# A list plan for the stretch between attention and the fast MLP tiles of a fused attention, Fourier-mixing and MLP kernel

## The chip, the cores and the metric

One core of one Trainium2 chip. The metric is device time in microseconds of one execution. Engines: TensorE (PE, with its weight loads PEld), VectorE (DVE), ScalarE (ACT), GpSimd (POOL) and SyncE (SP, which issues most DMAs).

## The reference

```python
bias = -(cum[:, :, :, None] - cum[:, :, None, :])         # cum: running sum of max(s, 0)
scores = where(causal, -1e9, q @ k.T / sqrt(64) + min(bias, 0))
x = softmax(scores) @ v                                   # 8 batches x 8 heads x 576 x 64
u = x + real(fft(fft(x, axis=seq), axis=model))           # 8 x 576 x 512
un = (u - mean(u)) / sqrt(var(u) + 1e-6)
out = u + max(un @ w_ch1, 0) @ w_ch2                      # 512 -> 2048 -> 512
```

All in float32; the kernel makes products nearly exact by splitting operands into a high and a low part and summing three products.

## The kernel before, in words

**Attention.** 32 pairs of heads (4 pairs for each of 8 batches). Iteration `i` of the loop at line 818 weaves the scores of pair `i`, the products with v of pair `i-1`, the row maxima (`pm`, line 685) of pair `i+1`, and, of earlier batches, the folds (`folds`, 470) and the Fourier products (`fourier`, 500: `pzs`, `pzc`, `pyc`, `pys`), whose result `u` goes to DRAM as `uD`. Each batch of 576 tokens becomes a run of rows of `uD`.

**MLP.** 4608 tokens in nine tiles of 512. A tile is normalised (`ln_tile`, 192), its four quarters split (`bh`, `bl`), and for each of 16 chunks `f` of the hidden 2048 there is a first product `h` (24 matmuls, 363), a relu split on ACT and DVE (`zh` 370, `zl` 371), and a second product into four PSUM accumulators (`acc`, 12 matmuls, 268 to 270). Tiles one and two run like that; tiles three to nine use a scheme with seven products in place of eight (`fast_tile`, 381, first matmul at 407).

**Weights** arrive as 64-bit numbers, in pieces of 128 x 256 (`raw`, 256 KB). A piece costs four DVE instructions (83, 85, 87, 88), one of ACT (84) and one of POOL (89), then a split into `wh` and `wl` (or, for the second matrix, `w2h` and `w2l`, whose split parts are kept in DRAM as `w2D` and loaded again for every tile). A chunk has four pieces, two of the first matrix and two of the second. Six chunks are converted in the shade of attention (`convert_w`), the other ten between the products of tiles one and two (`load_w`).

**Order.** Tiles one and two are cut in two phases because not all first matrices fit beside the Fourier buffers: chunks 0 to 7 of tile one, of tile two, then 8 to 15 of tile one, of tile two. The partial sum of the first phase goes through `uD` (`keeper`, 331: load, add, store). PE's order is that of the code: `weave` merges streams by rough shares. The other engines' orders are set by the framework's scheduler, which reorders within dependencies. All orders are fixed before the kernel starts.

## Time and profile before

| | |
|---|---|
| median of 3 runs | 1448.6 us (1447.39 to 1451.24) |
| profiled execution | 1449.54 us, its span 1447.8 |
| PE / DVE / ACT / POOL busy | 1291.8 / 865.7 / 630.1 / 523.3 us |
| mean granted TensorE clock | 0.954 |

Times in rows are microseconds from the span's start, durations of a single instruction in a group nanoseconds. In a group's row the part behind the second bar is idle time of the engine just before these instructions and what ended it. In a row of waits stand the total, the number and the longest. Matmuls overlap in the rows: the spacing of starts, not the length, is what one costs.

### The profile page before, as it was taken

The page shows a single profiled execution, that of the slowest core. Times are in us where ns is not written, and L with a number is a line of the kernel's source. Part 1 is how long each engine was busy: PE and PEld are TensorE (multiplying, and loading weights), DVE is VectorE, ACT ScalarE, POOL GpSimd, SP SyncE. Part 2 cuts the span into 40 slices and gives each one's busy share as a digit, 9 for nine tenths or more (in the row PEclk, how much of TensorE's full clock was granted, in tenths as well). Part 3 has the DMA queues.
Part 4 walks back from the last instruction along what each step waited for, and adds up shares of the span by engine and source line. Part 5 has one row for each costly group of instructions (what it writes and reads, how often), then busy time and mean ns, then how long its engine had stood idle before and what let it go on. Part 6 is the DMA issues. An engine that isn't in the chain of part 4 may idle for free.

```text
span 1447.8 us, 21997 instructions
## 1 busy us (share of the span) xinstructions
PE 1291.8 (89%) x7582; PEld 1124.5 (78%) x7582; DVE 865.7 (60%) x1989; ACT 630.1 (44%) x1472; POOL 523.3 (36%) x541
## 2 busy tenths in 40 slices
PE   4887979797988897488889989999999999999998
PEld 3676867686867685377769878888888898888987
DVE  6567676767676767586962778545445444554423
ACT  4665757566656556242431334333333333323321
POOL 6445464555556466544540444110211102021100
PEclk9998999898999998699989999999999999999999
DMA  8565556456655545446774433444435244452433
GB/s 198 139 179 148 140 159 180 132 156 180 154 165 142 166 123 184 170 144 200 225 239 146 137 135 103 147 132 129 161 103 185 92 146 146 124 168 88 140 123 116
DMA packets 130346, 218.68 MB, mean 151 GB/s; under 512 B 16985, under 2 KB 42009, under 8 KB 130235
## 3 DMA queue, kind: packets, MB, share of 16 engines
q1 hardware_dynamic: 127707, 213.18, 48.6%
q0 software_dynamic: 1712, 2.53, 0.9%
q10 hardware_dynamic: 816, 1.57, 0.3%
q8 instruction: 60, 0.98, 0.3%
q14 instruction: 51, 0.42, 0.1%
HBM read 159.72 MB, written 33.56 MB: 133 GB/s over the span
## 4 chain that ended last, share of the span: by engine, by line
PE 42%; DVE 7%; POOL 4%; DMA 4%; issue 4%; ACT 1%; SPq 0%; POOLq 0%; DVEq 0%; ACTq 0%
PE b L407 18%; PE acc L268 7%; PE acc L269 7%; PE acc L270 7%; DMA raw<-in_wP_dram 2%; PE h L363 1%; POOL we L89 1%; DMA w<-uD 1%; DVE wm L85 1%; DVE we L83 1%; DVE we L87 1%; DVE wm L88 1%; DMA u<-uD 1%; POOL w L315 1%; POOL t L216 0%
## 5 line engine op out<-in xcount | busy, mean ns | idle before, releaser
L268 PE MATMUL acc<-zh,w2h 128*128 128x512 f32 x576 | 230.4, 401 | 20.0 <-ACT zh L370 10.0
L270 PE MATMUL acc<-zl,w2h 128*128 128x512 f32 x576 | 230.6, 401 | 10.3 <-DVE zl L371 10.3
L269 PE MATMUL acc<-zh,w2l 128*128 128x512 f32 x576 | 231.3, 402 | 4.2 <-DMA w2l<-w2D 4.2
L749 PE MATMUL pavB<-P,va 128*128 128x320 f32 (+2 forms) x640 | 193.9, 397 | 10.0 <-ACT stage L753 9.6
L685 PE MATMUL pm<-KQ 128*128 128x256 f32 (+3 forms) x384 | 158.5, 432 | 44.2 <-DVE Mx L692 23.2
L721 ACT ACTIVATE P<-ps 128x320 f32<-128x320 f32 (+4 forms) x384 | 146.5, 393 | 117.2 <-PE ps L718 113.0
L315 POOL TENSOR_TENSOR w<-w,o 128x512 f32<-128x512 f32 x32 | 43.0, 1355 | 380.3 <-DVE o L311 342.7
L717 PE MATMUL ps<-KQ 128*128 128x256 f32 (+2 forms) x384 | 155.8, 408 | 19.7 <-ACT P L721 10.8
L692 DVE CUSTOM_DVE_ANT_0 trash<-pm,amask 128x128 bf16<-128x128 f32 (+3 forms) x256 | 123.7, 483 | 43.5 <-PE pm L685 26.9
L270 PEld LDWEIGHTS acc<-zl,w2h 128*128 128x128 f32 x576 | 110.4, 192 | 37.7 <-DVE zl L371 12.3
L268 PEld LDWEIGHTS acc<-zh,w2h 128*128 128x128 f32 x576 | 110.0, 191 | 29.0 <-ACT zh L370 10.5
L685 PEld LDWEIGHTS pm<-KQ 128*128 128x128 f32 x384 | 78.9, 208 | 65.2 <-DVE Mx L692 30.5
L749 PEld LDWEIGHTS pavB<-P,va 128*128 128x128 f32 x640 | 109.4, 200 | 19.3 <-ACT stage L753 14.1
L718 PE MATMUL ps<-Q,K 128*128 128x256 f32 (+2 forms) x384 | 121.9, 320 | 1.9 <-POOL Q L665 1.9
L399 ACT ACTIVATE zh<-cs 128x256 fp32r<-128x256 f32 x112 | 58.8, 525 | 142.8 <-DVE cs L419 88.7
L269 PEld LDWEIGHTS acc<-zh,w2l 128*128 128x128 f32 x576 | 110.7, 192 | 11.9 <-DMA w2l<-w2D 5.0
L665 POOL TENSOR_TENSOR Q<-qk,Q 64x576 fp32r<-64x576 f32 x64 | 100.2, 1580 | 39.8 <-DMA Q<-KQ 28.8
L717 PEld LDWEIGHTS ps<-KQ 128*128 128x128 f32 x384 | 77.5, 202 | 44.5 <-ACT P L721 17.0
L400 DVE SCALAR_TENSOR_TENSOR zl<-cs,zh 128x256 fp32r<-128x256 f32 x112 | 66.5, 594 | 69.2 <-ACT zh L399 69.2
L662 DVE TENSOR_TENSOR K<-qk,KQ 64x576 fp32r<-64x576 f32 x64 | 60.1, 940 | 75.9 <-ACT KQ L648 63.2
L407 PEld LDWEIGHTS b<-bh,wh 128*128 128x128 f32 x448 | 84.2, 189 | 24.3 <-DVE cs L419 4.8
L407 PE MATMUL b<-bh,wh 128*128 128x256 f32 x448 | 89.6, 281 | 3.5 <-DVE cs L419 3.5
(181 smaller groups left out, 2901.1 us busy)
## 6 DMA issues: line engine op xcount, KB each, us to landing
w2l<-w2D SPq DMA_DIRECT2D x136, 256.0 KB
w2h<-w2D SPq DMA_DIRECT2D x136, 256.0 KB
qk<-in_qkT_dram SPq DMA_DIRECT2D x32, 576.0 KB
raw<-in_wP_dram SPq DMA_DIRECT2D x64, 256.0 KB
...
```

Of the source, the lines that this page charges most:

```text
L268: nc.tensor.matmul(acc[j], a[:, cs], y, start=first, stop=False)
L269: nc.tensor.matmul(acc[j], b[:, cs], y, start=False, stop=False)
L270: nc.tensor.matmul(acc[j], a[:, cs], z, start=False, stop=final)
L400: nc.vector.scalar_tensor_tensor(out=y[1][:, at], in0=src, scalar=0.0, in1=y[0][:, at].bitcast(F32), op0=ALU.max, op1=ALU.subtract)
L407: nc.tensor.matmul(p[:, 0:256], a[:, j * 128:(j + 1) * 128], b[:, j], start=start and i == 0, stop=i == 5, skip_group_check=not start)
L665: nc.gpsimd.tensor_sub(q1[64:128, h], qk[0:64, h], q1[0:64, h].bitcast(F32))
L685: nc.tensor.matmul(p[:, :n], qy[:, h, 128 * c:128 * c + 128], ky[:, h, k0:k0 + n], start=True, stop=True)
L692: nc.vector.tensor_tensor_reduce(out=trash[:, :n], in0=p[:, :n], in1=amask[:, m0:m0 + n], scale=1.0, scalar=first if x else NEG, op0=ALU.a ...
L717: nc.tensor.matmul(p[:nk, :n], ky[:, h, ksl], qy[:, h, a:a + n], start=True, stop=False)
L718: nc.tensor.matmul(p[:nk, :n], k1[:, h, ksl], q1[:, h, a:a + n], start=False, stop=True)
L721: nc.scalar.activation(P[:nk, o:o + a + n - lo], p[:nk, lo - a:n], AF.Exp, scale=0.125)
L749: nc.tensor.matmul(p[:, a - lo:n], va[:nk, c, vs], P[:nk, o:o + w], start=c == 0, stop=c == cs[-1])
```

## The change

- Attention runs its loop for pairs 0 to 30, with all 24 pieces of the first six chunks spread over it and two buffers for them instead of one.
- Everything from pair 31 to the last chunk of tile two is written as generators. Each yields a step (engine, planned cost, what it needs, a buffer ring). `Flow.run` takes the step that can start first and, among those on its engine, the one with the earliest due time, and emits it. The plan's order is then kept on all engines; no scheduler reorders it.
- The first phase has six chunks (0 to 5) rather than eight. Conversion of chunks 6 to 15 is spread over the products. First halves of chunks 6 and 7 and all second halves have four staging buffers from attention's memory; first halves of chunks 8 to 15 have six, once the last Fourier is stored. Before there were three or four buffers.
- The first partial sum of tile one stays in four temporaries of the layer norm, with `u` added there; that of tile two is added to `u` in buffers fetched earlier and stays (three of four; one goes through `uD`).
- Tile one's `u` is loaded from SP's queue, not ACT's.

Three places in the order. The load of tile one's `u`: before, on ACT's queue among the exponentials (`P`) of pairs 30 and 31:

```order
L721 ACTIVATE P<-ps 128x320
L84 ACTIVATE we<-we,wbias 128x256
L753 COPY stage<-pavA 64x256
L721 ACTIVATE P<-ps 128x192
L721 ACTIVATE P<-ps 128x64
L195 DMA u<-uD 128x4x512
L69 CAST De_5887<-Df 128x289
```

Now, on SP's queue:

```order
L478 DMA uD<-xs 128x576
L695 DMA rb<-rd 64x576 x2
L625 DMA KQ_124<-mt 1x10x128
L477 DMA uD<-xa 128x2x576
L479 DMA uD<-xs 128x576
L683 DMA sums<-rows 16x1x36
L593 DMA va<-in_vA_dram 128x5x192
L1222 DMA u<-uD 128x4x512
L907 DMA rd<-sums 32x36
```

It moved behind three stores of `uD`, which wait for POOL, and behind the load of `va`, which waits for PE.

DVE where the late conversion begins. Before (`Do`, `De` belong to the last batch's fold, `wl` here are halves of chunks read back from DRAM):

```order
L371 SCALAR_TENSOR_TENSOR zl<-h,zh 128x512
L70 TENSOR_TENSOR Do_6480<-Df,Do_6479 128x288
L117 TENSOR_TENSOR wl_6561<-wl_6561,wh_6560 128x512
L482 TENSOR_TENSOR Df<-Aw 128x289
L117 TENSOR_TENSOR wl_6573<-wl_6573,wh_6572 128x512
L70 TENSOR_TENSOR De_6478<-Df,De_6477 128x289
L117 TENSOR_TENSOR wl_6585<-wl_6585,wh_6584 128x512
L486 TENSOR_TENSOR Df<-Bw 128x288
L83 TENSOR_SCALAR we<-raw 128x256
L85 TENSOR_SCALAR wm<-raw 128x256
```

Now:

```order
L955 TENSOR_TENSOR Do_6704<-Df,Do_6703 128x288
L980 TENSOR_TENSOR eh<-e,eh 1x289
L1110 TENSOR_SCALAR we<-raw 128x256 x2
L1301 SCALAR_TENSOR_TENSOR zl<-h,zh 128x512
L1267 RECIPROCAL r<-r 128x512
L1013 TENSOR_TENSOR zs_6878<-pz,zs_6877 96x256
```

Before, the first piece follows tile one's second `zl`; now it stands ahead of the sixth, and the first two instructions on a load are directly ahead of that `zl`.

DVE where the conversion ends. Before (`o` is an evacuation of an accumulator of tile two's first phase):

```order
L117 TENSOR_TENSOR wl_7587<-we,wh_7586 128x256
L338 TENSOR_TENSOR o<-r,acc_7641 128x512
L117 TENSOR_TENSOR wl_7587<-we,wh_7586 128x256
L83 TENSOR_SCALAR we<-raw 128x256
L85 TENSOR_SCALAR wm<-raw 128x256
L371 SCALAR_TENSOR_TENSOR zl<-h,zh 128x512
```

Now (`sx`, `s`, `sl` prepare the weights of the fast tiles):

```order
L1132 TENSOR_TENSOR wl_7339<-we,wh_7338 128x256
L1115 TENSOR_SCALAR wm<-raw 128x256
L1117 SCALAR_TENSOR_TENSOR wm<-raw,wm 128x256
L1120 SCALAR_TENSOR_TENSOR we<-raw,we 128x256
L1132 TENSOR_TENSOR wl_7341<-we,wh_7340 128x256 x2
L129 TENSOR_TENSOR sx<-sx 128x256
```

Before, the second halves of chunk 15 follow its `wl`, at the end of tile two's first phase; now `wl` of chunks 14 and 15 come last, after all second halves, with tile one in chunk 14.

```diff
-NC1 = 4.5
-N0 = 3
-N1 = 8
+N0 = 2
+N1 = 6
+NW = 8
+MARGIN = 1.5
+BACKLOG = 4.0
...
-    def keeper(t0, acc, r):
-        def done(j):
-            o = op.tile([128, TOK], F32, tag="o", name="o", bufs=2)
-            w = op.tile([128, TOK], F32, tag="w", name="w", bufs=3)
-            nc.sync.dma_start(out=w, in_=uD[j, :, t0:t0 + TOK])
-            nc.vector.tensor_mul(o, r, acc[j])
-            nc.gpsimd.tensor_add(w, w, o)
-            nc.sync.dma_start(out=uD[j, :, t0:t0 + TOK], in_=w)
-        return done
...
+    attb_ctx, attp_ctx, att_ctx, atop_ctx = (ExitStack() for _ in range(4))
     attb = attb_ctx.enter_context(tc.tile_pool(name="attb", bufs=1, side="right"))
-    psm = attb_ctx.enter_context(tc.tile_pool(name="psm", bufs=5, space=PSUM))
+    attp = attp_ctx.enter_context(tc.tile_pool(name="attp", bufs=1, side="right"))
...
-    weights = convert_w(attb, 0, NC, 1)
+    weights = convert_w(attb, 0, NC, 2)
...
+    for i in range(NP - 1):
...
+        share = NC * 4.0 / (NP - 1)
...
-            norm = chain(ln_tile(tiles[0], 6), plain(tiles[0]))
-            streams.append([take(norm, 10), 10 / 0.9])
...
-        for f in range(N0, N1):
-            yield from load_w(w1, f)
-        for _ in mixing:
-            yield 1.0
...
-    weave([plain_part(one, 0, N1, ready, early), N1], [chain(idle(1000), mixing), FOURIER * 0.6], [ahead(), 100],
-          [later(chain(ln_tile(two, 1), plain(two)), 2), 24])
...
-    STEPS = {(8, 0), (8, 3), (8, 4), (8, 5), (9, 2), (9, 3), (9, 4), (9, 5), *((10, x) for x in range(6)), (11, 0), (11, 1), (11, 3), (11, 5),
-             (12, 1), (12, 4), (12, 5), (13, 0), (13, 2), (13, 4), (14, 0)}
...
+    def piece(where, f, x, bufs, then):
+        e, rhold = yield dma(256, ring=(ring(where + "raw", bufs), 2))
+        home = stages[where]
+        raw = home.tile([128, 2 * WC], I32, tag="raw", name="raw", bufs=bufs)
+        nc.sync.dma_start(out=raw, in_=wP[f, :, WC * x:WC * x + WC].bitcast(I32))
+        hi = raw.rearrange("p (n w) -> p n w", w=2)[:, :, 1]
+        lo = raw.bitcast(U16).rearrange("p (n w) -> p n w", w=4)[:, :, 1]
+        e1, hold = yield ("DVE", 0.42, (e,), (ring(where + "we", bufs), 1))
+        n = home.tile([128, WC], I32, tag="we", name="we", bufs=bufs)
+        nc.vector.tensor_scalar(n, hi, 0x7FF00000, None, op0=ALU.bitwise_and)
+        e1 = yield act(400, e1)
+        nc.scalar.activation(n, n, AF.Relu, bias=wbias, scale=8.0)
+        _, mhold = yield ("DVE", 0.42, (e,), (ring(where + "wm", bufs), 1))
+        m = home.tile([128, WC], I32, tag="wm", name="wm", bufs=bufs)
+        nc.vector.tensor_scalar(m, hi, 0xFFFFF, 0x100000, op0=ALU.bitwise_and, op1=ALU.bitwise_or)
+        e = yield dve(256)
+        nc.vector.scalar_tensor_tensor(out=m.bitcast(F32), in0=lo, scalar=2.0 ** -16, in1=m, op0=ALU.mult, op1=ALU.add)
+        rhold.add(e)
+        e = yield dve(256, e1)
+        nc.vector.scalar_tensor_tensor(out=n, in0=hi, scalar=-0x80000000, in1=n, op0=ALU.bitwise_and, op1=ALU.bitwise_or)
+        rhold.add(e)
+        e = yield pool_(256, e)
+        nc.gpsimd.tensor_mul(n.bitcast(F32), m.bitcast(F32), n.bitcast(F32))
+        mhold.add(e)
+        yield from then(n.bitcast(F32), e, hold)
...
+            e = yield pool_(n, e) if pooled else dve(n, e)
+            (nc.gpsimd if pooled else nc.vector).tensor_sub(low[:, xs], v, h[:, xs].bitcast(F32))
...
+    def late_first(home, where, bufs, f0, f1):
+        for f in range(f0, f1):
+            wh = home.tile([128, 512], F32R, tag=f"wh{f}", name=f"wh{f}")
+            wl = home.tile([128, 512], F32R, tag=f"wl{f}", name=f"wl{f}")
+            W[f] = (wh, wl)
+            ready = Last(ev("W", f), 2)
+            for x in (0, 1):
...
+        e, hold = yield dma(1024, ring=(ring("lu", 1), 1))
+        u = lnp.tile([128, 4, TOK], F32, tag="u", name="u")
+        nc.sync.dma_start(out=u, in_=uD[:, :, t0:t0 + TOK].rearrange("c p t -> p c t"))
+        ev("lu", t0).hold = hold
...
+    parts = [(one_, 0, N1), (two_, 0, N1), (one_, N1, NF), (two_, N1, NF)]
+    last_of = [N1 - 1, 2 * N1 - 1, N1 + NF - 1, 2 * NF - 1]
+    todo = [(p, t0, f, f == f0, f == f1 - 1) for p, (t0, f0, f1) in enumerate(parts) for f in range(f0, f1)]
...
+    def evacuate(n, j, acc, e):
+        p, t0, f, _, _ = todo[n]
+        _, r = LN[t0]
+        if p:
+            e, ohold = yield ("DVE", 0.65, (e, ev("norm", t0)), (ring("oo", 2), 1))
+            o = op.tile([128, TOK], F32, tag="o", name="o", bufs=2)
+        else:
+            e, khold = yield ("DVE", 0.65, (e, ev("norm", t0)), (ring("lt", 4), 1))
+            o = lnp.tile([128, TOK], F32, tag="t", name="o", bufs=4)
+        nc.vector.tensor_mul(o, r, acc[j])
+        ev("acc", p, j).set(e)
+        if not p:
+            got, hold = yield dma(256, *at(*(("part", last_of[1], j) for j in range(4))), ring=(ring("oo", 2), 1))
+            w = op.tile([128, TOK], F32, tag="o", name="o", bufs=2)
+            nc.sync.dma_start(out=w, in_=uD[j, :, t0:t0 + TOK])
+            e = yield pool_(512, e, got)
+            nc.gpsimd.tensor_add(o, w, o)
+            hold.add(e)
+            kept[j] = (o, khold)
+            ev("part", n, j).set(e)
+            return
+        if p == 1:
+            yield wait(ev("fetched", j))
+            w, hold = ws[j]
+            e = yield pool_(512, e, ev("fetched", j))
+            nc.gpsimd.tensor_add(w, w, o)
+            ohold.add(e)
+            if j == 3:
+                e = yield dma(256, e)
+                nc.sync.dma_start(out=uD[j, :, t0:t0 + TOK], in_=w)
+                hold.add(e)
+            ev("part", n, j).set(e)
+            return
+        ev("rhold", t0).hold.add(e)
+        yield wait(ev("part", last_of[p - 2], j))
...
+                    flow.add(evacuate(n, j, acc[p], e), n - 900.0 + 0.1 * j)
...
+        for n, (p, t0, f, first, final) in enumerate(todo):
+            yield wait(ev("W", f), ev("plain", t0))
+            wh, wl = W[f]
+            bl = BL[t0]
+            e, hold = yield pe(12 * mm(256), ev("W", f), ev("plain", t0), ring=(ring("ps", 3), 1))
+            h = bank("h")
...
+            flow.add(relu_flow(h, hold, e, n), n - 900.5)
+            if n:
+                yield from second_product(n - 1)
...
+        yield wait(ev("out", L), *(ev("wD", f) for f in range(NC)))
+        attb_ctx.close()
+        stages["stage2"] = stage_ctx.enter_context(pool("stage2"))
+        late_first(w1, "stage2", 4, N1, NW)
+        flow.add(late_second(), 55.0)
+        yield wait(ev("u", B))
         fft_ctx.close()
         wB = ctx.enter_context(pool("wB", side="right"))
         op = ctx.enter_context(pool("op", side="right"))
...
+        late_first(wB, "stage3", 6, NW, NF)
...
+    for i in (L - 2, L - 1, L):
+        flow.add(close_pair(i), 3.0 + 8.0 * (i - L + 2))
+    flow.add(fourier_flow(B - 1, 14.0), 14.0, 1.0)
+    flow.add(folds_flow(B, 28.0), 28.0, 0.5)
+    flow.add(fourier_flow(B, 40.0), 40.0, 1.0)
+    flow.add(second_tile(), A0)
+    flow.add(fetch_u(), A0 + 60.0)
+    flow.add(second_loads(), mlp_due(N1) - 12.0, 1.87)
+    flow.add(mlp(), A0, 2.8)
+    flow.add(prepare(three_, C0 + 44.0), C0 + 44.0, 1.0)
+    flow.run(ev("first"), ev("prepared"), ev("sums_w"))
+    BL.pop(one_), BL.pop(two_)
     PLACES = {(0, 1), (1, 1), (1, 3), (1, 4), (1, 5), (2, 0), (2, 1), (2, 2), (2, 3), (2, 4), (2, 5), *((3, k) for k in range(7)),
...
+class Flow:
+    LAG = {"PE": 0.3, "ACT": 0.22, "DVE": 0.15, "POOL": 0.15}
+    def __init__(self):
+        self.free = dict.fromkeys(("PE", "ACT", "DVE", "POOL", "SP"), 0.0)
+        self.wire = 0.0
+        self.live = []
+    def add(self, gen, due, step=0.0):
+        self.send([gen, due, step, None], None)
+    def send(self, s, got):
+        new = s[3] is None
+        try:
+            s[3] = s[0].send(got)
+        except StopIteration:
+            if not new:
+                self.live.remove(s)
+            return
+        s[1] += s[2]
+        if new:
+            self.live.append(s)
+    def start(self, step):
+        engine, _, deps, ring = step
+        t = self.free[engine] if engine else 0.0
+        if ring:
+            deps = (*deps, ring[0].next())
+        late = MARGIN if engine == "SP" else 0.0
+        for d in deps:
+            if d.t is None:
+                return None
+            t = max(t, d.t + late)
+        return t
+    def run(self, *goals):
+        while any(g.t is None for g in goals):
+            ready = [(t, s) for s in self.live for t in (self.start(s[3]),) if t is not None]
+            if not ready:
+                raise RuntimeError("the plan is stuck: " + str([(s[0].__qualname__.split(".")[-1], s[1]) for s in self.live]))
+            t, s = min(ready, key=lambda x: (x[1][3][0] is not None, x[0]))
+            engine = s[3][0]
+            t, s = min(((u, v) for u, v in ready if v[3][0] == engine and u <= t + 0.05), key=lambda x: x[1][1])
+            self.place(s, t)
+    def place(self, s, t):
+        engine, cost, _, ring = s[3]
+        if engine == "SP":
+            self.wire = max(self.wire, t + 0.6) + 0.1 + cost / 250.0
+            self.free[engine] = max(t + 0.6, self.wire - BACKLOG)
+            e = Event(self.wire + 2.2 + MARGIN)
+        elif engine:
+            self.free[engine] = t + cost
+            e = Event(t + cost + self.LAG[engine])
+        else:
+            e = Event(t)
+        self.send(s, (e, ring[0].take(ring[1])) if ring else e)
+def pe(cost, *deps, ring=None):
...
+def act(n, *deps, ring=None):
+    return "ACT", 0.03 + n * 0.00095, deps, ring
...
+def dve(n, *deps, ring=None):
+    return "DVE", 0.1 + n * 0.0014, deps, ring
...
+def pool_(n, *deps, ring=None):
+    return "POOL", 0.15 + n * 0.0024, deps, ring
...
+def mm(n):
+    return 0.012 + n / 2150
...
```

More of the change, by code (lines that the diff above doesn't have):

```diff
@@ new lines, in prepare @@
+    def prepare(t0, due):
+        yield wait(ev("plain", two_), ev("norm", two_), *at(*(("part", last_of[2], j) for j in range(4))))
+        flow.add(norm_flow(t0, at(*(("acc", 2, j) for j in range(4)))), due, 0.8)
+        yield wait(ev("norm", t0))
+        ready = Last(ev("prepared"), 7)
+        e0 = ev("norm", t0)
+        for k, _ in enumerate(combine(t0)):
+            e0 = yield ("DVE", 1.2, (), None)
+        for k in range(7):
+            yield from block_flow(t0, k, SRC[t0][k], ready, e0)
@@ new lines, in fused_kernel @@
+    lnp = bp = w2p = zp = accp = hx = op = cp = sp = sx = None
+    flow.free.update(ACT=1.0, DVE=2.0, POOL=2.0)
+    for name, t in {("row",): 5.0, ("sums", L - 2): 2.0, ("x", L - 2): 1.0, ("out", L - 3): 0.0, ("out", L - 4): 0.0, ("folded", B - 1): 4.0, ("out", 4 * B): 0.0}.items():
+        ev(*name).t = t
+    for h in range(2):
+        ev("P4", L - 1, h).t = ev("P5", L - 1, h).t = 1.0 + h
+    for f in range(NC):
+        ev("wD", f).t = 2.0
+    flow.add(tail(), 0.0)
+    flow.add(av_flow(L - 1, 0.0), 0.0)
```

771 lines of the change are left out of this document (613 added, 158 removed).

## The prediction

> **What bounds the kernel now.** I first read the page's slices of the span (busy tenths, 36.2 us each, and the granted TensorE clock under them), then the windows by stage.
>
> ```profile
> span 1447.8 us, 21997 instructions
> ...
> PE   4887979797988897488889989999999999999998
> ...
> PEclk9998999898999998699989999999999999999999
> ```
>
> Slice 17 stands out: PE at 4 tenths, clock at 6. Before it lies attention, after slice 23 PE is at 9. The windows cut this at events: 533.6 is the end of the last row-maximum matmul (the same PE row, 2010, in both kernels), 836.3 the first matmul of the third tile (line 407, in the view of that line). Columns are length, busy time of PE, weight loads, DVE, ACT and POOL with counts, granted clock, DMA share, GB/s.
>
> ```profile
> 100.00:533.60 433.60, 373.65 (x2102) 316.50 (x2103) 306.01 (x908) 270.46 (x674) 237.99 (x252) 0.93 0.56 155
> ...
> 533.60:836.30 302.70, 246.32 (x1430) 215.09 (x1430) 197.66 (x374) 109.46 (x235) 138.03 (x140) 0.89 0.55 179
> 533.60:587.70 54.10, 40.29 (x198) 33.85 (x198) 39.99 (x70) 31.59 (x74) 33.72 (x30) 0.81 0.58 183
> 587.70:630.30 42.60, 21.38 (x117) 17.49 (x115) 31.31 (x51) 15.27 (x31) 21.13 (x19) 0.72 0.51 169
> 668.00:749.50 81.50, 65.44 (x367) 56.55 (x366) 71.70 (x161) 33.22 (x73) 41.81 (x50) 0.90 0.75 233
> 760.00:836.30 76.30, 74.35 (x474) 66.71 (x473) 34.76 (x46) 18.25 (x32) 19.76 (x19) 1.00 0.42 140
> 836.30:1447.80 611.50, 601.06 (x3733) 537.87 (x3731) 300.07 (x524) 193.49 (x439) 95.54 (x80) 1.00 0.40 132
> ```
>
> ```profile
> L407 PE MATMUL b<-bh,wh x448: 274/280/416, 836.3 to 1434.4; 128*128 128x256 f32 x150
> ```
>
> The tiles after 836.3 (42% of the span) are full: 601 of 611.5 us at full clock, and the change leaves them alone. The stretch it rewrites is not. At full clock its 246.3 us of PE are 246.32 x 0.89 = 219 us, so 302.7 - 219 = 84 us are lost there, some 27 us to the low clock and 56 us to idle time. Two pieces are worst: 587.7 to 630.3, where PE works half the time, and 668 to 749.5, where DVE has 71.7 of 81.5 us (88%) and PE follows it. Whom PE waits for:
>
> ```profile
> PE acc L270 <- DVE zl L371: 10.3, 4, 6.6
> PE acc L268 <- ACT zh L370: 10.0, 1, 10.0
> PE acc L268 <- DVE o L338: 7.8, 4, 4.4
> ```
>
> The 10.0 us is one wait: the first tile's first relu stands on ACT behind tile two's layer norm. This is order, not work.
>
> **The change part by part.** I follow three milestones to the first matmul of tile three: the first `zl` (relu remainder of tile one, chunk 0), the low half of chunk 15's first matrix (`wl15`, without which no later first product can run), and the end.
>
> *Attention.* All 24 conversion pieces of the first six chunks now run before 533.6, where 20 did. Four pieces more:
>
> ```profile
> L85 DVE TENSOR_SCALAR wm<-raw 128x256 int32<-128x256 int32 x44 | 24.1, 549 | 0.6 <-DMA raw<-in_wP_dram 0.6
> L371 DVE SCALAR_TENSOR_TENSOR zl<-h,zh 128x512 fp32r<-128x512 f32 x32 | 21.9, 684 | 49.8 <-ACT zh L370 49.7
> L87 DVE SCALAR_TENSOR_TENSOR we<-raw,we 128x256 int32<-128x256 int32 x44 | 21.9, 497 | 0.9 <-ACT we L84 0.9
> L88 DVE SCALAR_TENSOR_TENSOR wm<-raw,wm 128x256 f32<-128x256 uint16 x44 | 20.0, 456 | 0.5
> L83 DVE TENSOR_SCALAR we<-raw 128x256 int32<-128x256 int32 x44 | 18.1, 411 | 12.5 <-DMA raw<-in_wP_dram 12.2 <-DMA wD<-we 0.2
> L237 DVE TENSOR_TENSOR bl<-u,bh 128x512 fp32r<-128x512 f32 x12 | 11.6, 997 | 0.4 <-ACT bh L235 0.4
> L222 DVE RECIPROCAL r<-r 128x512 f32<-128x512 f32 x3 | 10.0, 3345 | 2.0 <-ACT r L220 2.0
> L117 DVE TENSOR_TENSOR wl<-we,wh 128x256 fp32r<-128x256 f32 x20 | 9.9, 494 | 3.8 <-ACT wh L115 3.7
> ```
>
> A piece is 0.411 + 0.549 + 0.456 + 0.497 = 1.91 us of DVE, four are 7.6 us. Attention has DVE at 306 of 433.6 us (71%) and the order of PE there is unchanged, so most is covered: between 0 and +7.6, I take **+2**; without that cover it is all 7.6.
>
> *Head, to the first `zl`.* Before, DVE reaches it at 615.8 (last row below). The new order puts it behind a chain that starts with tile one's 1 MB load. That load was on ACT's queue; now it is on SP's, behind the `uD` stores of batch 5 and the load of `va`, which left at:
>
> ```profile
> 550.28 0.60 SPq L668 DMA_DIRECT2D va<-in_vA_dram  x1
> ```
>
> So it leaves near 551, not in time for a landing at 545.5 as now (542.44 + 3.04 below). The links after it, from the chain of waits, and for tile two's norm from ACT's and DVE's timelines:
>
> ```profile
> 542.44 3.04 DMA u<-uD
> ...
> 594.09 1.23 POOL t L198
> ...
> 597.47 0.81 PE mu L185
> ```
>
> ```profile
> 607.11 0.62 ACT L179 CAST th<-t 128x512 fp32r<-128x512 f32 x1 [1.64 <-POOL t L216]
> ...
> 628.90 0.69 ACT L220 ACTIVATE r<-var,eps 128x512 f32<-128x512 f32 x1
> ```
>
> ```profile
> 607.76 0.69 DVE L181 TENSOR_TENSOR tl<-t,th 128x512 fp32r<-128x512 f32 x1
> ...
> 615.83 0.67 DVE L371 SCALAR_TENSOR_TENSOR zl<-h,zh 128x512 fp32r<-128x512 f32 x1
> ```
>
> Landing 551 + 3 = 554. From the first sum (594.09) to the second `th` (607.11) tile two took 13.0 us. Then `th` 0.62, `tl` 0.69, the variance matmuls 0.8, root 0.69, reciprocal 3.35, and the first `zl` 0.68: 6.8 us. 554 + 13.0 + 6.8 = 574, and I add 4 for the rest of the attention pair on the same engines: **578**. If everything that stood between in the old order stayed between, it would be 616; if the load kept its place, 545.5 + 13.0 + 6.8 + 4 = 569. PE is no bound here: the head's share is less than the 40.29 x 0.81 = 33 us that it does by 587.7 now.
>
> *From `zl` to `wl15`.* DVE rows in the new order between the two: 40 pieces x 1.91 = 76.5; 20 half-width `wl` at 0.494 and the full ones 13.7; 20 `zl` x 0.684 = 13.7; `bl` 4.0 and the rest of tile two's norm 10 (3.35 of it the reciprocal); fold and Fourier of the last batch, evacuations and one scaling 24 (estimates from the groups of the same lines, each below 6 us in this stretch). Together 142. The groups of the stretch add up to 219 us where DVE is busy 197.66, since neighbours overlap: x 0.90 = 128 us. In the conversion window DVE is busy 88%: 128 / 0.88 = 145 us, so `wl15` at **723**. Bounds: 128 with DVE never idle (706), and the old pace, a rival below. The two groups of PE instructions that this competes with:
>
> ```profile
> 633.44 0.23 PE acc L270
> ...
> 649.92 2.87 PE h L363 x24
> ```
>
> A chunk of one tile is 24 first-product matmuls, 2.87 us, and 12 x 0.23 = 2.76 us of second product, 5.63. By `wl15` PE has 20 chunks, 113 us, and some 15 us of Fourier and norm: 128 us, as much as DVE. The balance is what the reordering buys, and neither can be much behind the other.
>
> *To the end.* From `wl15` 11 first products (31.6), 11 second products (30.4) and tile three's norm matmuls (0.9): 63 us, by the 97% of the row 760 to 836.3 (74.35 of 76.3): 65. First matmul of tile three at **788**, before 836.3.
>
> *Partial sums.* Of the evacuations' 16 loads and 8 stores of 256 KB in tiles one and two, 9 loads and one store stay: 14 transfers fewer, 3.7 MB. They lie in DMA time at 55% share, so they are free but for the 7.8 us that PE waited for `o`; that is inside my 88%. The accumulators still change hands three times.
>
> Sum: -48 + 2 = -46. Profiled execution 1449.54 us (span 1447.8 and 1.7 around it), 0.9 over the median 1448.6: **1403**.
>
> The clock weighs against this where DVE sets the pace, as PE then idles a little in every chunk:
>
> ```profile
> 740.00:750.00 10.00, 7.16 (x41) 6.00 (x40) 8.69 (x20) 3.73 (x8) 4.67 (x6) 0.87 0.87 280
> 600.00:610.00 10.00, 1.65 (x3) 0.83 (x3) 8.33 (x9) 5.79 (x11) 4.65 (x3) 0.50 0.32 112
> ```
>
> A DVE-paced window costs 0.13 of the clock, a stall of 10 us half of it. The three densest chunks have four pieces, three `wl` and a `zl` of DVE: 7.6 + 1.5 + 0.7 = 9.8, by 0.90 / 0.88 some 10 us. At 0.87 a chunk's PE takes 6.5 us, so this costs nothing. [...]
>
> DVE and POOL also slow each other. The same instruction takes:
>
> ```profile
> 623.03 0.28 DVE L85 TENSOR_SCALAR wm<-raw 128x256 int32<-128x256 int32 x1
> ...
> 624.14 1.38 DVE L85 TENSOR_SCALAR wm<-raw 128x256 int32<-128x256 int32 x1
> ```
>
> The mean of 549 ns holds a mix of both. POOL is busy 138 of 302.7 us (46%) and would be at some 53% of the shortened stretch; if the excess over 0.28 grows in that ratio, 40 pieces cost 40 x 0.27 x 0.15 = 1.6 us more. [...]
>
> **The rivals.**
>
> *PE becomes the bound.* The order lets DVE convert ahead and the whole stretch runs like 760 to 836.3. For it: DVE's 198 us fit into 226. Against: DVE and PE need the same 128 us in the middle, with handoffs each way in every chunk. 219 / 0.97 = 226, -77 + 2: **1375**.
>
> *Conversion keeps its pace.* From its first piece to `wl15` it now takes:
>
> ```profile
> 622.83 0.28 DVE L83 TENSOR_SCALAR we<-raw 128x256 int32<-128x256 int32 x1
> ...
> 744.16 0.43 DVE L117 TENSOR_TENSOR wl<-we,wh 128x256 fp32r<-128x256 f32 x1 [0.46 <-ACT wh L115]
> ```
>
> 122 us, a hole included where buffers wait for the last Fourier. In the new order 30 us of DVE stand between `zl` and the first piece: 578 + 31 + 122 + 65 = 796, **1411**. For it: chunks 8 to 15 still wait for that memory. Against: the second halves no longer do. If the head gains half only (597), it ends at **1430**.
>
> *Head-of-line blocking, slower.* DVE's queue is fixed; now `we<-raw` pairs stand directly ahead of a `zl`, so a late load holds the relu and with it PE. Late loads exist, five in the chain of waits:
>
> ```profile
> 663.80 4.46 DMA raw<-in_wP_dram
> ...
> 741.51 6.11 DMA raw<-in_wP_dram
> ```
>
> It decides from 46 / 40 = 1.15 us of new delay per piece. A third of 40 pieces at 5.3 us would be 71 us: **1474**. Against: now the waits are 12.2 us in all, with 3 or 4 buffers; the change has 4 and 6, and less to move.
>
> *It doesn't do what it says:* the planner's durations miss so far that stalls eat the gain, **1449**.
>
> **How the numbers follow.** Forecast 1390 to 1422 (with the kept pace at 1411): 0.60. PE-bound, below 1390: 0.21. Half a head, 1422 to 1444: 0.10. No change: 0.03. Slower: 0.06. The range leaves out a tenth on either side: **1376 to 1430**. Within 0.3% (4.3 us) is what this kernel's measurement can't tell from no change: faster 0.91, same 0.03, slower 0.06.
>
> **What would show it.** First `zl` near 578, `wl15` near 723, tile three's first matmul near 788, 533.6 moved by 0 to 8. DVE near 90% and POOL over 50% from 610 to 720, clock at 0.9 there and 1.0 after. It is wrong if DVE waits for `raw` by more than 40 us in all, if the first `zl` comes after 600, or if attention grew by more than 8 us.

## The result, and the profile after

The changed kernel took 1430.5 us (median of 4 runs, 1428.1 to 1433.1), the kernel before 1448.0; the ratio is 0.988, 95% interval 0.985 to 0.990. The change gains 17.5 us where 46 were forecast, and the time lies just above the range. The profiled run took 1428.06 us. First the page's slices (36 us each), PE and the granted clock:

```profile
span 1426.3 us, 21949 instructions
...
PE   4886979797979898889879989999999999999998
...
PEclk9999999898999999999979999999999999999999
```

The hole in slice 17 of the old page is gone. What is left is a dent in slices 20 and 21 (PE 8 and 7, clock 7 in slice 21). Cut at the milestones of the prediction (last row maximum, first `zl`, `wl15`, first matmul of tile three; columns as there):

```profile
100.00:541.20 441.20, 373.88 (x2094) 316.54 (x2093) 312.25 (x912) 269.23 (x671) 238.65 (x252) 0.94 0.56 155
541.20:587.50 46.30, 36.83 (x217) 31.77 (x215) 30.94 (x51) 30.63 (x72) 26.52 (x26) 0.96 0.50 169
587.50:741.00 153.50, 132.76 (x792) 119.48 (x793) 137.94 (x261) 57.37 (x127) 86.03 (x93) 0.91 0.62 206
741.00:813.90 72.90, 69.46 (x425) 62.08 (x425) 34.74 (x49) 18.50 (x32) 21.01 (x21) 0.97 0.45 147
813.90:1426.30 612.40, 601.25 (x3733) 538.02 (x3731) 296.98 (x522) 193.24 (x438) 95.92 (x80) 1.00 0.40 131
680.00:741.00 61.00, 46.94 (x263) 41.69 (x262) 60.24 (x120) 23.61 (x54) 36.89 (x42) 0.87 0.58 186
```

The last row is the dent: from 680 on DVE is busy for 60.24 of 61 us, and PE follows it. Against the prediction:

| Stage | Forecast | Measured | Miss |
|---|---|---|---|
| attention, last row maximum against 533.5 | +2 | +7.7 | 5.7 |
| to the first `zl`, the attention's delay taken off | 578 | 579.8 | 1.8 |
| `zl` to `wl15` | 145 | 153.5 | 8.5 |
| `wl15` to tile three | 65 | 72.9 | 7.9 |
| the tiles after | 611.5 | 612.4 | 0.9 |

These 24.8 us are the distance between the forecast span (1401.8) and 1426.3, but for rounding. So three terms are to be explained: the attention, the middle (first `zl` to `wl15`), and the end (`wl15` to tile three).

DVE's groups between the first `zl` and `wl15`, the four rows of a conversion piece and the relu remainder:

```profile
L1117 DVE SCALAR_TENSOR_TENSOR wm<-raw,wm 128x256 f32<-128x256 uint16 x40 | 24.5, 613 | 1.2
L1120 DVE SCALAR_TENSOR_TENSOR we<-raw,we 128x256 int32<-128x256 int32 x40 | 21.0, 528 | 0.0
L1110 DVE TENSOR_SCALAR we<-raw 128x256 int32<-128x256 int32 x40 | 20.1, 526 | 0.0
L1115 DVE TENSOR_SCALAR wm<-raw 128x256 int32<-128x256 int32 x40 | 19.3, 484 | 0.0
L1301 DVE SCALAR_TENSOR_TENSOR zl<-h,zh 128x512 fp32r<-128x512 f32 x20 | 13.6, 680 | 5.1 <-ACT zh L1299 5.0
```

No idle time of DVE before them is put down to a `raw` load; before, it was 12.2 us. A piece is now 0.613 + 0.528 + 0.526 + 0.484 = 2.15 us, not 1.91. In the attention, PE's waits for the row maxima between 100 and 526 us, of the kernel before (lines 685 and 697):

```profile
PE pm L685 <- DVE Mx L692: 19.1, 9, 4.3
...
PE pmt L697 <- DVE Mx L692: 8.5, 6, 3.4
```

and of the changed kernel:

```profile
PE pm L610 <- DVE Mx L617: 24.4, 14, 4.4
PE pmt L622 <- DVE Mx L617: 18.1, 11, 3.4
```

27.6 us became 42.5. And at the end, PE's first waits around `wl15` (741.0), with the clock below them:

```profile
739.29 0.80 PE L1433 MATMUL h<-bh,wl 128*128 128x256 f32 x2 [3.08 <-DVE wl L1132]
...
751.05 0.50 PE L1413 MATMUL acc<-zh,w2h 128*128 128x512 f32 x1 [1.10 <-ACT zh L1299]
...
753.59 0.51 PE L1415 MATMUL acc<-zl,w2h 128*128 128x512 f32 x1 [1.81 <-DVE zl L1301]
```

```profile
735.00:740.00 5.00, 1.92 (x7) 1.63 (x8) 4.92 (x12) 2.02 (x5) 2.56 (x4) 0.50 0.22 66
740.00:745.00 5.00, 5.00 (x21) 4.62 (x21) 1.98 (x3) 0.41 (x1) 2.73 (x4) 0.50 0.38 124
745.00:750.00 5.00, 4.96 (x33) 4.40 (x31) 2.99 (x5) 0.73 (x2) 3.62 (x6) 0.98 0.93 315
```

### The profile page after: what moved, and what is told of

It reads as the page before. It is cut to its first block, busy times and chain, and to the rows that moved or that the text cites. A ratio compares the mean times of both kernels' runs of the same rounds, so it can differ in the third digit from the quotient of the medians.

```text
span 1426.3 us, 21949 instructions
## 1 busy us (share of the span) xinstructions
PE 1285.1 (90%) x7582; PEld 1122.4 (79%) x7582; DVE 878.1 (62%) x1989; ACT 627.8 (44%) x1472; POOL 522.1 (37%) x541
## 4 chain that ended last, share of the span: by engine, by line
PE 48%; DVE 8%; POOL 2%; issue 1%; ACT 1%; DMA 1%; SPq 0%; POOLq 0%; DVEq 0%; ACTq 0%
PE b L331 19%; PE acc L242 7%; PE acc L243 7%; PE acc L244 7%; PE h L1433 3%; PE acc L1415 1%; PE acc L1414 1%; PE acc L1413 1%; DVE wm L1117 1%; DVE we L1120 1%; DVE we L1110 1%; DVE wm L1115 1%; DVE wl L1132 1%; PE pz L1005 1%; DVE zl L1301 1%
## 5 line engine op out<-in xcount | busy, mean ns | idle before, releaser
L646 ACT ACTIVATE P<-ps 128x256 f32<-128x256 f32 x372 | 141.7, 393 | 121.6 <-PE ps L643 117.6
L674 PE MATMUL pavB<-P,va 128*128 128x320 f32 x600 | 180.8, 394 | 9.4 <-ACT stage L678 9.4
L242 PE MATMUL acc<-zh,w2h 128*128 128x512 f32 x452 | 179.0, 396 | 0.0
L243 PE MATMUL acc<-zh,w2l 128*128 128x512 f32 x452 | 179.0, 396 | 0.0
L244 PE MATMUL acc<-zl,w2h 128*128 128x512 f32 x452 | 178.4, 395 | 0.0
L642 PE MATMUL ps<-KQ 128*128 128x256 f32 x372 | 148.7, 403 | 14.6 <-ACT P L646 5.8
L643 PE MATMUL ps<-Q,K 128*128 128x256 f32 x372 | 117.1, 318 | 2.1 <-POOL Q L590 2.1
L324 DVE SCALAR_TENSOR_TENSOR zl<-cs,zh 128x256 fp32r<-128x256 f32 x112 | 65.9, 588 | 69.2 <-ACT zh L323 69.2
L642 PEld LDWEIGHTS ps<-KQ 128*128 128x128 f32 x372 | 74.6, 201 | 37.6 <-ACT P L646 11.1
L244 PEld LDWEIGHTS acc<-zl,w2h 128*128 128x128 f32 x452 | 85.3, 189 | 20.4 <-DVE zl L324 0.4
L331 PE MATMUL b<-bh,wl 128*128 128x256 f32 x448 | 90.2, 283 | 0.0
L331 PE MATMUL b<-bl,wh 128*128 128x256 f32 x448 | 89.6, 281 | 0.0
```

The costliest lines, as they stand in the source:

```text
L242: nc.tensor.matmul(acc[j], a[:, cs], y, start=first, stop=False)
L243: nc.tensor.matmul(acc[j], b[:, cs], y, start=False, stop=False)
L244: nc.tensor.matmul(acc[j], a[:, cs], z, start=False, stop=final)
L324: nc.vector.scalar_tensor_tensor(out=y[1][:, at], in0=src, scalar=0.0, in1=y[0][:, at].bitcast(F32), op0=ALU.max, op1=ALU.subtract)
L331: nc.tensor.matmul(p[:, 0:256], a[:, j * 128:(j + 1) * 128], b[:, j], start=start and i == 0, stop=i == 5, skip_group_check=not start)
L642: nc.tensor.matmul(p[:nk, :n], ky[:, h, ksl], qy[:, h, a:a + n], start=True, stop=False)
```

## The experiments

Times are medians; ratios are to the kernel before, which was timed beside each group of runs (1449.5, 1452.4, 1448.3 and 1448.5 us beside e1 to e4, e5 to e8, e9 to e12 and e13 to e15).

### The attention: e1, e2, e3, e15

e1 gives the kernel before the change's quota of pieces:

```
-        share = NC1 * 4.0 / (NP - 2) if i < NP - 2 else (1.0, 4.0)[i - NP]
+        share = NC * 4.0 / (NP - 1)
```

> The kernel before, with all 24 pieces of the first six chunks converted inside the attention's pairs as the change has them (20 before; the other four ran after the last row maximum). Nothing else is changed. Theory A, the attention pays DVE's full price for each extra piece: the last row-maximum matmul moves from 533.5 to 541 (four pieces x 1.91 us), and since four pieces go from the head, where DVE is not always busy, the whole comes out 0 to 7 us above 1448. Rival B, the four pieces find cover as I forecast (+2) and the 7.7 us of the change come from something else in its attention (the second buffer, the other order near the end): the last row-maximum at 534 to 536, and the whole within 3 us of 1448 or below it.

Measured: last row maximum at 538.3 (+4.8), 1454.2 us, ratio 1.003 (1.001 to 1.006). The edit alone moves the last row maximum to between the two theories, and the whole by as much (4.7 us). e2 leaves out the last four of the changed kernel's 24 pieces:

```
-                m = yield from rounded(pool, f, x, bufs)
+                if f < 5:
+                    m = yield from rounded(pool, f, x, bufs)
+                else:
+                    raw = pool.tile([128, 2 * WC], I32, tag="raw", name="raw", bufs=bufs)
+                    nc.sync.dma_start(out=raw, in_=wP[f, :, WC * x:WC * x + WC].bitcast(I32))
+                    yield 0.8
```

> The changed kernel, where chunk 5's four pieces are loaded but not converted (their DVE, ACT and POOL work is left out and an earlier piece is stored in their place, so chunk 5's weights are wrong numbers). Theory A: the last row-maximum goes back from 541.2 to about 533.6, and the whole from 1430.5 to 1423. Rival B, something else in the attention costs the 7.7 us: 539 to 541 still, and 1428 to 1431.

Measured: 540.7, and 1426.9 us. The four pieces do not account for the 7.7: the last row maximum hardly moves without them. So theory A falls. (The whole is 3.6 us below the changed kernel's, but its four runs, 1420.3 to 1430.3, overlap with those.) e3 keeps all 24 and spreads them:

```
-        streams.append([take(weights, share), share + 1e-9])
+        streams.append([even(i), share + 1e-9])
+    def even(i):
+        while spread_[0] < NC * 4.0 * (i + 1) / (NP - 1) - 0.3:
+            c = next(weights, None)
...
```

> The changed kernel, with its 24 pieces spread evenly over all 31 pairs; in the changed kernel each pair takes a whole piece, so they are done by about pair 25. Theory A, price by count and not by place: the last row-maximum stays at 540 to 542 and the whole at 1429 to 1432. Rival P, the place makes the price (a whole piece in each pair is more than the slack of a pair, three quarters of one is not): the last row-maximum at 534 to 537, the whole 1424 to 1427.

Measured: 534.4, and 1424.8 us, ratio 0.984 (0.980 to 0.988). The place makes the price. One profiled run gives the last row maximum only to some 3 us, but the two ways of placing the pieces do not overlap: the seven profiled kernels of this study with these 24 pieces spread evenly have it at 530.8 to 536.4, the four with the changed kernel's attention at 540.0 to 544.9. `take` lets a pair run until its quota of 0.77 is reached or passed, and a piece has four steps of 0, 0.4, 0.4 and 0.2, so that nearly every pair took a whole piece, and 24 were done by about pair 25. The start of the row-maximum transpose in some pairs (one per pair, from PE's timeline):

| Pair | before | e3, even | after | e11 |
|---|---|---|---|---|
| 14 | 243.6 | 246.6 | 246.0 | 260.2 |
| 19 | 328.9 | 331.4 | 341.1 | 349.4 |
| 25 | 435.0 | 437.7 | 446.6 | 463.3 |
| 31 | 536.3 | 537.2 | 544.0 | 566.5 |

The changed kernel loses 12 us by pair 19 and gets back less than half once its pieces are done. With the even spread PE's waits for row maxima are, in the same window:

```profile
PE pm L610 <- DVE Mx L617: 20.6, 9, 4.0
PE pmt L622 <- DVE Mx L617: 12.7, 9, 3.4
```

33.3 us, between 27.6 and 42.5. e15 asks whether the price is DVE's own time or POOL's multiply beside it:

```
-        nc.gpsimd.tensor_mul(e.bitcast(F32), m.bitcast(F32), e.bitcast(F32))
         yield 0.4
```

> The changed kernel (1430.5) without POOL's multiply in the 24 pieces of the attention; they stay at a whole piece per pair (the multiply is left out, so the first six chunks' weights are wrong numbers). Theory C, POOL beside DVE is what the attention pays for: the last row maximum at 534 to 537 in place of 541.2, the waits of PE for row maxima (42.5 us between 100 and 526) back to 30 to 34, the whole 1423 to 1426. Theory Q, DVE's own 1.9 us for a piece delay the row maxima: 539 to 542, 38 to 43 us, 1428 to 1431.

```profile
PE pm L609 <- DVE Mx L616: 21.4, 19, 4.9
PE pmt L621 <- DVE Mx L616: 18.7, 14, 3.5
```

Measured: 40.1 us of waits, the last row maximum at 544.1, 1432.3 us. POOL's multiply is not the cause, though the last row maximum and the whole lie a little beyond theory Q's bounds. What is left is the rest of a piece, of which DVE's 1.9 us stand on the engine that PE waits for; its ACT step and its load were not tried apart, nor was where in a pair a piece stands.

### The middle: e4, e6, e8, e10

e4 takes POOL's multiply out of the 40 late pieces:

```
         e = yield pool_(256, e)
-        nc.gpsimd.tensor_mul(n.bitcast(F32), m.bitcast(F32), n.bitcast(F32))
```

> The changed kernel without POOL's multiply in each of the 40 late pieces (the plan still has its place, the instruction is not there, and the weights of chunks 6 to 15 are wrong numbers). Theory C, DVE's rows are long because POOL works beside them: the four rows of a piece go from 526, 484, 613 and 528 ns to below 450 on the mean, DVE does its work between the first zl and wl15 in 128 us or less in place of 138, wl15 comes 8 to 12 us earlier after the first zl than 153.5, and the whole is 1419 to 1424. Rival O, the order sets the pace and DVE's longer rows only fill its waits: DVE's busy time falls, its idle time grows by as much, zl to wl15 stays at 150 to 154, and the whole at 1427 to 1431.

DVE's groups between its first `zl` (591.7) and its `wl15` (735.2), and the window itself:

```profile
L1120 DVE SCALAR_TENSOR_TENSOR we<-raw,we 128x256 int32<-128x256 int32 x40 | 20.5, 514 | 0.0
L1117 DVE SCALAR_TENSOR_TENSOR wm<-raw,wm 128x256 f32<-128x256 uint16 x40 | 20.0, 501 | 1.2
L1110 DVE TENSOR_SCALAR we<-raw 128x256 int32<-128x256 int32 x40 | 16.7, 442 | 0.0
L1300 DVE SCALAR_TENSOR_TENSOR zl<-h,zh 128x512 fp32r<-128x512 f32 x20 | 13.7, 684 | 9.8 <-ACT zh L1298 9.7
L1115 DVE TENSOR_SCALAR wm<-raw 128x256 int32<-128x256 int32 x40 | 13.4, 336 | 0.0
```

```profile
591.70:735.20 143.50, 128.77 (x792) 115.94 (x793) 122.14 (x261) 55.86 (x128) 54.89 (x54) 0.96 0.67 219
```

The middle is 143.5 in place of 153.5, the whole 1422.9, ratio 0.983 (0.979 to 0.987). A piece's four rows are 1.79 us, 448 ns on the mean; two of them stayed above the 450 that I expected. POOL has 31.1 us less (86.03 to 54.89), and DVE's rows of 40 pieces are 14.3 us shorter: 0.46 us of DVE per us of POOL. The multiply also leaves each piece's chain, so not every us of the 10 needs to be contention; the shorter rows are.

e6 and e8 move work between the two, on the evenly spread kernel; the first diff is e6's (remainders to POOL), the second e8's (multiply to DVE):

```
-                flow.add(piece(where, f, x, bufs, split_w(wh, wl, slice(WC * x, WC * x + WC), WC, False, ready)), late_due(f) - 20.0 + x)
+                flow.add(piece(where, f, x, bufs, split_w(wh, wl, slice(WC * x, WC * x + WC), WC, True, ready)), late_due(f) - 20.0 + x)
```

```
-        e = yield pool_(256, e)
-        nc.gpsimd.tensor_mul(n.bitcast(F32), m.bitcast(F32), n.bitcast(F32))
+        e = yield dve(256, e)
+        nc.vector.tensor_mul(n.bitcast(F32), m.bitcast(F32), n.bitcast(F32))
```

> The evenly spread kernel with the remainders of the late first halves (20 wl rows of 0.57 us on DVE) given to POOL. Theory L, DVE's amount of work alone: 11 us less on DVE in the middle, wl15 8 to 11 us earlier after the first zl than 153, the whole 1414 to 1418. Theory C, what POOL does is paid by DVE: POOL's 20 rows of 0.89 us are 18 us more beside DVE; at the rate of the run without the multiply (14 us of DVE for 32 of POOL) they cost DVE 8 us, so wl15 comes 0 to 4 us earlier and the whole is 1421 to 1426.

> The evenly spread kernel with the multiply of each of the 40 late pieces on DVE in place of POOL. Theory C, POOL's work beside DVE lengthens DVE's rows: DVE gets 40 x 0.4 = 16 us more, its other rows give 14 back, zl to wl15 stays at 150 to 157 us, the whole at 1422 to 1429. Theory L, no such price: DVE's rows keep their length, zl to wl15 becomes 165 to 170 us, the whole 1437 to 1441.

The same row in e6, and then in e8:

```profile
L1124 DVE TENSOR_SCALAR wm<-raw 128x256 int32<-128x256 int32 x40 | 23.6, 590 | 0.0
```

```profile
L1124 DVE TENSOR_SCALAR wm<-raw 128x256 int32<-128x256 int32 x40 | 13.1, 327 | 0.0
```

In e6 a piece's four rows grow to 2.40 us, +10 over 40 pieces, which takes back what the 20 rows gave: 1424.6 us against 1424.8. In e8 they are 1.81 us, 14 back for the multiply's 19.2: 1425.2 us. POOL's busy time in the middle went from 85.85 us to 100.18 in e6 and to 59.23 in e8, so the price was 0.7 us of DVE per us of POOL in the one and 0.5 in the other. So theory C stands in the rows and in the whole of both. Its milestone does not: I expected `wl15` 0 to 4 us earlier in e6, and it came 158.5 after the first `zl` in place of 152.9; in e8 162.3. The end shrank by as much or nearly (71.0 and 65.1 us in place of 74.4). The time of the last piece is thus not what paces the stretch: PE had got on further by then.

The whole contention story has a control in the rows above. The relu remainder `zl` reads one operand from PSUM, and stays at 680 to 685 ns in all of these kernels. Of the rows that read `raw` and a second tile, `wm<-raw,wm` varies (613 ns, 501 without the multiply); `we<-raw,we` hardly moved on the mean (528 and 514). `wm<-raw` and `we<-raw` read one tile, and vary as well (484 and 336, 526 and 442). In the changed kernel (shortest, median and longest in ns):

```profile
L1115 DVE TENSOR_SCALAR wm<-raw x40: 274/284/1377, 630.4 to 739.2; 128x256 int32<-128x256 int32 x40
```

What sets the rows that vary apart from `zl`, no run here shows.

e10 sets the plan's durations to the measured means, on the kernel of the late sums (e7, below):

```
-        _, mhold = yield ("DVE", 0.42, (e,), (ring(where + "wm", bufs), 1))
+        _, mhold = yield ("DVE", 0.49, (e,), (ring(where + "wm", bufs), 1))
...
-        e = yield dve(256, e1)
+        e = yield ("DVE", 0.53, (e1,), None)
```

> The kernel of the late sums (1419.8), with the plan's durations of the conversion's rows set to the means that the changed kernel showed (DVE 0.53, 0.49, 0.61 and 0.53 in place of 0.42, 0.42, 0.46 and 0.46, the remainders 0.57 and 1.2, ACT 0.51). The program is the same, the list is another. Theory D, the plan drifts since it takes DVE's rows for too short, and the wrong order costs part of the middle's 8.5 us: 3 to 8 us shorter, 1412 to 1417. Rival K, the work sets the pace and a truer list has no more to gain: 1417 to 1423; longer too, since the list is greedy.

Measured: 1422.2 us, ratio 0.982 (0.979 to 0.984), against 1419.8 and 0.979 (0.975 to 0.983). A truer list is no better: rival K.

### The end: e7, e12

The steps that form the block sums wait in the plan for later relus, once on the evenly spread kernel and once on the changed kernel as it is:

```
-                e = yield (("DVE", "DVE", "DVE", "DVE", "ACT", "DVE")[k], 0.9, (), None)
+                e = yield (("DVE", "DVE", "DVE", "DVE", "ACT", "DVE")[k], 0.9, (ev("Z", 23 + k // 2 + 2 * g),), None)
```

> The evenly spread kernel where the 12 steps that make the block sums of the weights for the third tile wait, in the plan, for the relus of chunks 23 to 28 of the list of 32, so that none stands on DVE directly behind wl15. Theory S, the steps ahead of a relu remainder cost the end its excess (PE waited 1.4 and 1.9 us there, and ran at half clock before): from wl15 to the third tile 70 to 71 us in place of 74.4, the whole 1420 to 1422. Rival W, it is PE's own work (12 chunks left and not 11): 73 to 75 us as now, the whole 1424 to 1426.

> The changed kernel with the late sums alone; its pieces in the attention stay as they are. Theory S: from wl15 to the third tile 68 to 70 us in place of 72.9, the whole 1425 to 1427. Rival V, the gain seen with the even spread was another state of the list and not the sums: 72 to 74 us, 1429 to 1432.

DVE's timeline of the changed kernel right behind `wl15`:

```profile
740.70 1.28 DVE L1132 TENSOR_TENSOR wl<-we,wh 128x256 fp32r<-128x256 f32 x2
745.84 0.94 DVE L129 TENSOR_TENSOR sx<-sx 128x256 f32<-128x256 f32 x1 [3.85 <-POOL sx L123]
...
750.54 1.20 DVE L143 TENSOR_TENSOR sl<-s,sh 128x768 fp32r<-128x768 f32 x1 [0.90 <-ACT sh L141]
...
752.85 0.68 DVE L1301 SCALAR_TENSOR_TENSOR zl<-h,zh 128x512 fp32r<-128x512 f32 x1
```

and of e7:

```profile
740.64 1.28 DVE L1141 TENSOR_TENSOR wl<-we,wh 128x256 fp32r<-128x256 f32 x2
744.11 0.69 DVE L1310 SCALAR_TENSOR_TENSOR zl<-h,zh 128x512 fp32r<-128x512 f32 x1 [2.19 <-ACT zh L1308]
```

The first `zl` behind `wl15` comes 10.9 us after the end of the last `wl` (740.70 + 1.28) in the one and 2.2 us after it in the other: nine sum steps, one of which waited 3.85 us for POOL, stood in front of it. The end takes 69.2 us in both e7 and e12, and the whole 1419.8 and 1426.2: 5.0 and 4.3 us off. In six profiled kernels that keep the sums where the change has them (the changed kernel, e2, e3, e4, e9 and e15) the end takes 72.8 to 74.6 us. Theory S, in both; e7 went a little beyond its bounds.

### The traffic: e9

```
+        if p == 0 or p == 1 and j < 3:
+            for x in range(2):
+                nc.sync.dma_start(out=spare[8 * p + 2 * j + x], in_=wD[x, :, 0:512])
```

> The changed kernel with 14 further transfers of 256 KB on SP's queue, two at each of seven evacuations of the first two parts (copies from one DRAM buffer to another that nothing waits for), in place of the 14 that the change saved. Theory N, as forecast, those transfers cost no time: the whole at 1428 to 1433. Rival T, the transfers are near their limit between the first zl and wl15 (0.96 of the DMA time for 20 us there): 3.7 MB at 322 GB/s are 11 us, and half of it or all comes on top: 1436 to 1442.

Measured: 1430.5 us, ratio 0.988 (0.985 to 0.991), the same as without them; from the last row maximum to tile three it is 274.3 us where the changed kernel has 272.7. Theory N: the saved transfers are worth nothing that these runs can tell from noise. What keeping the partial sums in SBUF does to the order of the evacuations was not tried apart.

### Seven chunks, and a version that beats both: e5, e11, e13, e14

e5 sets NC = 7 and N1 = 7 on the evenly spread kernel; e11 adds the late sums and gives every fourth pair a third of the others' pieces.

> The evenly spread kernel (1424.8, milestones 534.4, 584.4, 737.3, 811.7) with seven chunks in the first phase in place of six: 28 pieces converted inside the attention, 36 late, seven chunks in each of the first two parts. Theory L, the amount of DVE work between the first zl and wl15 is what binds: four pieces (4 x 2.15) and two half remainders less, a full one (1.2) more, so about 8 us off DVE there, and the third tile 7 to 10 us earlier after the last row maximum than 277.3; 0.9 pieces a pair in the attention costs 0 to 4 there; the whole 1415 to 1422. Rival O, the listed order binds and not the amount: the stretch from the last row maximum to the third tile stays within 3 us of 277, the whole at 1424 to 1430.

> Seven chunks in the first phase, late sums, and the 28 pieces kept away from every fourth pair (the one where the fold begins gets a third of what the others get). Theory F, the attention's loss with seven chunks (last row maximum at 543.9 with 28 pieces spread evenly, 534 to 536 with 24) comes where pieces meet the fold: 536 to 540 now, and with a stretch of 268 less the 5 of the late sums the third tile begins at 799 to 803, the whole 1411 to 1416. Rival G, 0.9 pieces a pair are more than the attention can hide wherever they stand: 543 to 546 again, the whole 1417 to 1425.

e5: the stretch from the last row maximum to tile three is 268.1 us in place of 277.3, as theory L has it, but the attention takes 9.5 more (543.9), and the whole is 1430.7 us. e11: 265.5 us of stretch, but the last row maximum at 563.7 and 1442.2 us. Both my theories missed that: 1.09 pieces in three pairs of four (28 / 30.8 x 1.2) cost far more than 0.9 in all of them (last column of the table above). Keeping away from the fold did not help. That a pair can hide only so much fits both, but what sets the limit was not tried.

e13 and e14 put the four pieces of chunk 6 where DVE idles, between the last row maximum and the first relu, and leave the attention its 24:

```
-NC = 6
+NC = 7
...
-N1 = 6
+N1 = 7
...
-    weights = convert_w(attb, 0, NC, 2)
+    weights = convert_w(attb, 0, 6, 2)
...
+        for x in range(4):
+            flow.add(piece("attb", 6, x, 2, store(x)), 15.0 + 3.0 * x)
```

This is e14; e13 has 10.0 for 15.0. `store` writes a converted piece to `wD`, from where chunk 6 is loaded as the six before it.

> The kernel of the late sums (1419.8) with chunk 6 moved out of the middle: its four pieces are converted between the last row maximum and the first relu, in the plan from 10 us on, and seven chunks make the first two parts. The attention keeps its 24 pieces. Theory L, the middle is bound by DVE's amount of work and the head has DVE time to spare (33 of 50 us busy): last row maximum at 534 to 537, 0 to 4 us more in the head, and the third tile 5 to 9 us earlier after the last row maximum than 274.4; the whole 1411 to 1416. Rival O, what leaves the middle comes back in the head, on the chain to the first relu: the stretch stays at 272 to 277 us, the whole at 1418 to 1423.

> The same with the four pieces 5 us later in the plan, which lists the stretch 4 us shorter again. Theory L: 1409 to 1415, no longer than the one with the earlier pieces by more than 2 us. Rival O: the pieces then stand in front of the first relus, 1418 to 1425.

The three windows of e14 (last row maximum at 534.1, `zl` 591.1, `wl15` 733.5, tile three 794.0):

```profile
534.10:591.10 57.00, 41.41 (x217) 35.41 (x215) 41.20 (x66) 32.27 (x76) 33.31 (x31) 0.85 0.55 179
591.10:733.50 142.40, 131.72 (x843) 118.72 (x844) 130.79 (x255) 56.65 (x125) 80.20 (x88) 0.99 0.67 220
733.50:794.00 60.50, 59.39 (x374) 53.22 (x373) 33.81 (x47) 17.57 (x30) 22.24 (x21) 1.00 0.47 156
```

The head grows by 6.2 us over e7's 50.8, the middle shrinks by 12.0 (from 154.4) and the end by 8.7 (from 69.2): 259.9 us where e7 has 274.4. e13 needs 266.8. The wholes are 1415.7 us, ratio 0.978 (0.975 to 0.982), and 1407.8 us, ratio 0.973 (0.969 to 0.977). Theory L holds, and e14 came out a little below its bound. Why the same four pieces, planned 5 us later, are worth 7.9 us more was not tried apart. It is the fastest kernel of this study: with the even spread, the late sums and the seventh chunk in the head, three edits of the list give 22.7 us beyond the change.

## Why the prediction was wrong

Three terms of the sum were too small, each for a reason of its own: the attention by 5.7 us, the middle by 8.5 and the end by 7.9. The head and the tiles after came within 1.8 us. None of the signs of being wrong that I had named came: DVE waited for no `raw`, the first `zl` came at 587.5, and the attention grew by 7.7 us.

**Attention, +2: the step that failed is "most is covered".** I read the cover from an average, 71% of DVE's time over 434 us. The price is made in each pair that takes a whole piece (PE's waits for row maxima are 42.5 us so, 33.3 with the even spread). e3 shows that the cover was there for the same 24 pieces, spread (+0.9 in its profiled run), and e1 and e2 together that what each pair takes costs, and not the four more. I had the quota's line in the diff and did not work out how many pieces a pair takes. The upper bound that I kept, 7.6 as DVE's full price, met the 7.7 by chance: it was derived from the four pieces, and e2 shows that these are not it.

**Head, 578: right in its sum, with two errors that nearly cancel.** The load of tile one lay behind the stores and the load of `va` as forecast, but by the chain of waits it left at 555.9 and took longer:

```profile
555.93 6.20 DMA u<-uD
562.20 0.10 issue
562.29 1.69 POOL t L1227
```

With the attention's 7.7 us passed on, my 551 would be 558.7: the load left 2.8 us before that, and took 3.2 us more than my 3.0. It landed at 562.1, and the chain behind it took 25.4 us where I had 24.

**Middle, 145: the term is DVE's 142 us of rows, which I priced at the durations of the trace of before.** DVE was busy for 137.9 us in place of 128, at 90% of the stage (88% forecast). The 40 pieces make 84.9 us in place of 76.5, that is 8.4 of the 10 us. I had the mechanism, and sized it at 1.6 us by scaling with POOL's share (46% to 53%). Where the 40 pieces stand, POOL's share did go from 49% to 55%, but DVE's went from 76% to 92%. The windows from the first piece to `wl15`, of the kernel before and of the changed one:

```profile
622.80:744.20 121.40, 104.47 (x637) 92.40 (x635) 91.99 (x212) 46.15 (x103) 59.14 (x70) 0.94 0.62 194
```

```profile
624.60:741.00 116.40, 102.34 (x615) 92.43 (x614) 107.62 (x222) 44.59 (x102) 64.36 (x75) 0.91 0.63 207
```

POOL has only 5.2 us more here, which at e4's 0.46 would be 2.4 us. What grew more is the time in which both work at once: added up from the timelines of the two engines, 46.9 us before and 61.0 now. My scaling left out that a DVE with little idle time meets POOL more often. From `zl` to `wl15` e4 took this time from 77.7 to 48.6 us and 14.3 us off the rows, 0.49 for each. As an estimate by that price, 14.1 us more make some 7 of the 8.4; no run changed the overlap by itself. DVE paid 0.5 to 0.7 us for each us of POOL (0.46 in e4, 0.5 in e8, 0.7 in e6), and my scaling had no such price in it.

**End, 65: I counted 11 chunks where PE had 12, and left out the sums.** At `wl15` PE was still in the first product of the list's chunk 20, counted from 0 (chunk 14 of tile one), since chunks 14 and 15 became ready close together: PE's wait for the one ended at 739.29, the other's last `wl` began at 740.70. 11.6 first products (33.3), 12 second ones (33.1) and the norm (0.9) are 67.3 us, 4.3 above my 63; the half clock until 745 adds some 2 and gives PE's 69.46 us. The rest is waits: the block sums ahead of a `zl`, worth 3.7 us of the end by e12.

**The clock.** I had three dense chunks at 0.87, at no cost. The last 61 us before `wl15` do have 0.87 on the mean, but as a mix of full and half clock: PE ran at 0.50 from 735 to 745, after a gap of 2.07 us and with one of 3.08 in it. What it cost in the middle, where PE waits for DVE in any case, was not measured; behind `wl15` it is some 2 us, an estimate from the row of 740 to 745 (5.00 us of PE at 0.50).

**The rivals.** Head-of-line blocking on late loads did not come: DVE waited for no `raw` at all. "Conversion keeps its pace" with half a head, 1430, names the time that came, but not its course: the head was not half, it came within 2 us. Its middle, though, is what came: 31 and 122 us make 153, and the first piece of the changed kernel began 37.1 us after the first `zl`, `wl15` 116.4 us after that, 153.5 in all.

```profile
L1110 DVE TENSOR_SCALAR we<-raw x40: 278/290/1384, 624.6 to 738.1; 128x256 int32<-128x256 int32 x40
```

The change thus took 5 us from the pace of conversion (121.4 before). The rival's reason, buffers that wait for the last Fourier, did not hold: DVE was busy for 92% of these 116.4 us. The PE-bound case (1374 by its own sum, not 1375) fell, as DVE had 99% of the last 61 us before `wl15`. The traffic saved on the partial sums gave no time that shows, as forecast (e9).
